# Light convolution and maxout MLP on one core: tokens loaded with their predecessors in one transfer, and a shorter weight split

## The chip, the cores and the metric

The kernel runs on one core of a Trainium2 chip. The metric is device time in microseconds (us) of one execution; the median of three runs of the kernel before is 1700.21 us (1697.39 to 1700.39). Engines are called as in the profile: PE (TensorE matmul) and PEld (its weight loads), DVE (VectorE), ACT (ScalarE), POOL (GpSimd), SP (SyncE, which here issues transfers and passes on waits).

## The reference

Inputs are `x` (8 x 4160 x 192) and `weight_gen` (8 x 4160 x 8 heads x 7 taps), 32-bit floats, and the weights `w1`, `w2`, `w3` (192 x 768) and `w_out` (768 x 192), which arrive as 64-bit floats.

```python
w = exp(weight_gen - max(weight_gen)); w = w / (sum(w) + 1e-9)       # over the 7 taps
out[b, s, h*24+g] = sum_k w[b, s, h, k] * x_pad[b, s + k, h*24+g]     # x_pad: 6 zero rows ahead of each batch
h = maximum(maximum(out @ w1, out @ w2), out @ w3)                    # 33280 tokens
result = h @ w_out
```

Each token is a weighted sum of itself and the six tokens before it in its batch, then a two-layer net with the maximum of three products as its nonlinearity.

## The kernel before, in words

**Tiling.** The 33280 tokens are laid on 128 partitions, 260 consecutive tokens on each, so that 16 partitions hold one batch. The work goes through 65 chunks of 4 tokens a partition (512 tokens). Loads and softmax are done by *super chunks*: super 0 is chunk 0 alone, each later one has three chunks. `load_super` (L183) brings a super's `weight_gen` rows and its tokens with the 6 preceding ones. For all supers but the first two the preceding tokens are on the same partition and one transfer of 128 rows brings everything (L191). In super 0 (and for two of the six in super 1) they are the last tokens of the partition before: a transfer of the super's own tokens (L197), 8 transfers of 15 partitions each for the rows ahead (L202), and a memset to zero (L196) for the partitions with which a batch begins.

**Stages of a chunk.** `softmax` (L210): maximum and sum on DVE, subtraction and multiplication on POOL, Exp on ACT. `product` (named x*c*.*t*, L246): on POOL, tap weights times tokens of token column *t*. `total` (+*c*.*t*, L261): sum over the taps on DVE. `transpose` (t*c*): channels onto partitions, by PE for chunks 0 to 2 (L276, L277), by DVE and ACT later. `parts` (p*c*, L300 to L309): the transposed values are split in a high and a low part in the reduced format that PE multiplies in. `up` (L343): for each of 9 steps (3 pairs of column blocks times 3 matrices) two accumulators of 9 products for each half of the 128 rows of PE; the three matrices' results are combined by a copy (ACT, L376) and two maxima (DVE, L378), then split in `h_hi` (ACT, L381) and `h_lo` (POOL, L385). `down` (L389): the second layer, 4 column blocks, for the chunk before.

**Splitting the weights.** The 64-bit weights are taken as pairs of 32-bit words. `split` (L453) makes from one unit of them a high and a low 32-bit float: |high word| on ACT (L470), a copy of the middle half words (L476), then DVE clamps (L481), shifts and masks (L483), puts the sign in (L488); ACT rounds to the high part (L493); DVE masks out the low mantissa (L494) and the exponent (L495), ACT scales the low part (L497) and POOL multiplies (L498). Units: a0 to a8 (256 elements; pair *jp* and matrix *i*), b0 to b2 (384 elements; the last 64 of the 192 input rows, whose high part ACT copies to both halves of `wb_hi`, L553, four copies a unit), d0 to d5 (192 elements, `w_out`). All of it happens while chunks 0 and 1 already run.

**Order.** The program is written out tick by tick: 22 ticks a chunk, 18 with half a step of `up` each and 4 (ticks 12 to 15) with `down` products. From chunk 5 on a table gives the tick of each stage. Before that, the list `OPENING` (L27) says at which tick which stage is issued, from -1 (before the first product); `stage` (L581) issues the next piece of it and, before that, whatever it depends on; `finish` issues the rest of a stage when it is due: p*c*, a*k* and b*k* at their step, all d at tick 34. Each engine works through its instructions in the order in which they are issued, so one that waits holds up all behind it on that engine. PE's accumulators, the transposed values and the split's work tiles share 8 PSUM banks (tag `ph`). A half of PE starts after a `nop` on SP has seen the other half's last product (L340), so SP's queue is on PE's way too. Loads go out on SP in program order (L558 to L566): s0 a0 b a1 s1 a2 d, the letters standing for a super, a pair's three matrices and the rest.

Of the kernel before, what the change touches and what calls it, by code (L numbers as in the profile page):

```python
# [13 lines left out]
F32 = mybir.dt.float32  # L14
F32R = mybir.dt.float32r
U32 = mybir.dt.uint32
U16 = mybir.dt.uint16
AF = mybir.ActivationFunctionType
ALU = mybir.AluOpType
# [4 lines left out]

OPENING = {  # L27
    -1: (
        "x0.0 x0.1 a0 a0 a1 a0 a1 x0.3 a2 a0 x0.2 a2 +0.0 a2 b0 b0 s1 +0.1 a1 a2 b0 +0.3 s1 "
        "a1 b0 s0 b1 +0.2 s1 a3 a3 a6"  # L30
    ),
    0: "a6 a3",
    1: "a6 b1 a5 t0 +1.0 a4 x1.2",
    2: "s0",
    3: "a3 x1.0 b1 a6 b2 a5",
    4: "a4 a5 t0",
    5: "a4 x1.1",
    6: "t0",
    7: "s0",
# [69 lines left out]
):  # L109

# [18 lines left out]


    assert NT % TC == 0
    chunks = [(t, TC) for t in range(0, NT, TC)]
    supers = [[0]]
    for c in range(1, len(chunks)):
        if len(supers) == 1 or len(supers[-1]) == SC:
            supers.append([])  # L150
        supers[-1].append(c)
# [18 lines left out]


    F_MAX = float(np.array(0x47EFFFFF, np.uint32).view(np.float32))
    F_MIN = float(np.array(0x38000000, np.uint32).view(np.float32))
    NU = 3 * P
    halves = (slice(0, DB), slice(DB, P))
    state = {}

    def pin(ins):

        tc.keep_in_program_order(ins)  # L180
        return ins

    def load_super(s):  # L183
        cs = supers[s]
        a = chunks[cs[0]][0]
        n = sum(chunks[c][1] for c in cs)
        xt = sup.tile([P, TS + PAD, D], F32, name="xt")
        wt = sup.tile([P, TS, H * K], F32, name="wt")
        pin(nc.sync.dma_start(out=wt[:, :n], in_=wf[:, a : a + n]))
        if a >= PAD:  # L190
            pin(nc.sync.dma_start(out=xt[:, : n + PAD], in_=xf[:, a - PAD : a + n]))  # L191
        else:


            z = PAD - a
            pin(nc.vector.memset(xt[:, :z], 0.0))  # L196
            pin(nc.sync.dma_start(out=xt[:, z : n + PAD], in_=xf[:, : a + n]))  # L197
# [8 lines left out]
        state["x", s], state["w", s], state["n", s] = xt, wt, n  # L206

    def softmax(s):  # L210
# [12 lines left out]
        yield  # L223
        pin(nc.vector.tensor_reduce(den, w3v, axis=AX.X, op=ALU.add))
        pin(nc.vector.tensor_scalar_add(den, den, 1e-9))
        pin(nc.vector.reciprocal(den, den))
        yield
# [6 lines left out]
    def product(c, t):  # L234
# [22 lines left out]
    def total(c, t):  # L257

        r = state.pop(("r", c, t))
        pin(  # L260
            nc.vector.tensor_reduce(  # L261
                state["acc", c][:, t], r, axis=AX.X, op=ALU.add
            )
        )

    def transpose(c):


# [42 lines left out]

    def after(ins, other):
# [26 lines left out]
    def up(step, half):  # L343
# [3 lines left out]
        for odd in range(2):  # L347
            j = 2 * jp + odd
            terms = [(wa_hi[:, j, i], xa_hi), (wa_hi[:, j, i], xa_lo), (wb_hi[:, j, i], xb)]
            if half == odd:  # L350
# [69 lines left out]

    clock = [0.0, 0.0]
# [25 lines left out]


    words = [w.bitcast(U32) for w in (w1, w2, w3, w_out)]

    def split(raw, hi, lo):  # L453

        high = raw[..., 1]


        n = int(np.prod(raw.shape[1:-1]))
        if 2 * n <= CH:
            both = ps.tile([P, CH], F32, name="ph")  # L460
            u, l = both[:, :n], both[:, n : 2 * n]
        else:
            u, l = (ps.tile([P, CH], F32, name="ph")[:, :n] for _ in range(2))
        e, f = (prep.tile([P, NU], F32, name=name, bufs=3)[:, :n] for name in ("e", "f"))
        f_words = f
        if len(raw.shape) == 4:
            u, l, e, f = (v.rearrange("p (i n) -> p i n", n=P) for v in (u, l, e, f))
        ui, li, ei = (v.bitcast(U32) for v in (u, l, e))

        pin(nc.scalar.activation(u, high.bitcast(F32), AF.Abs))  # L470
        yield


        flat = raw.rearrange("p i n w -> p (i n) w") if len(raw.shape) == 4 else raw
        pin(
            nc.scalar.copy(  # L476
                f_words.bitcast(U16).rearrange("p (n h) -> p n h", h=2),
                flat.bitcast(U16)[..., 1:3],
            )
        )  # L480
        pin(nc.vector.tensor_scalar(u, u, F_MAX, F_MIN, op0=ALU.min, op1=ALU.max))  # L481
        pin(
            nc.vector.tensor_scalar(  # L483
                ui, ui, 3, 0x3FFFF000, op0=ALU.logical_shift_left, op1=ALU.bitwise_and
            )
        )
        pin(
            nc.vector.scalar_tensor_tensor(  # L488
                ui, high, 0xC0000000, ui, op0=ALU.bitwise_and, op1=ALU.bitwise_or
            )  # L490
        )
        yield
        pin(nc.scalar.copy(hi, u))  # L493
        pin(nc.vector.tensor_scalar(li, f.bitcast(U32), 0x01FFFFFE, None, op0=ALU.bitwise_and))  # L494
        pin(nc.vector.tensor_scalar(ei, ui, 0xFF800000, None, op0=ALU.bitwise_and))  # L495
        yield
        pin(nc.scalar.activation(f, li, AF.Copy, scale=2.0**-36))  # L497
        pin(nc.gpsimd.tensor_tensor(lo, f, e, op=ALU.mult))  # L498


# [39 lines left out]
    def prepare_a(u):  # L540

        jp, i = divmod(u, 3)
        raw = raws_a[jp][:, i].rearrange("p (j n) w -> p j n w", j=2)
        pair = slice(2 * jp, 2 * jp + 2)
        yield from split(raw, wa_hi[:, pair, i], wa_lo[:, pair, i])

    def prepare_b(jp):
        raw = raw_b[:, jp]
        hi = prep.tile([P, 3, P], F32R, name="hi", bufs=1)
        yield from split(raw, hi, wb_lo[:, jp])  # L550
        for odd, h in enumerate(halves):
            for to in halves:
                pin(nc.scalar.copy(wb_hi[to, 2 * jp + odd], hi[h].bitcast(F32)))  # L553

    def prepare_down(j):
        yield from split(raw_down[:, j], wo[:, j, :D], wo[:, j, D:])

    state["now"] = -1  # L558
    load_super(0)
    load_up(0)  # L560
    load_rest()
    load_up(1)
    load_super(1)
    load_up(2)
    load_down()
    make_identity(nc, ident)  # L566


# [56 lines left out]
    for s, cs in enumerate(supers):  # L625
        ticks(cs[0], f"s{s}", SOFTMAX)
        if s > 1:
            at(max(TICKS * (cs[0] - LOAD[0]) + LOAD[1], 0), lambda s=s: load_super(s))
# [7 lines left out]
    for c in range(NC + 1):  # L636
        for tick in range(TICKS):
# [3 lines left out]
            if 2 * DOWN_AT <= tick < 2 * DOWN_AT + TC:  # L641
                if c == 1:
                    for j in range(NJ):
                        finish(f"d{j}")
                if 0 < c < NC:
# [5 lines left out]
            if odd == 0 and c == 0:  # L651
                finish(f"a{k}")
                finish(f"b{k // 3}")
            if c == NC:


# [48 lines left out]
```

## Time and profile before

| | before |
|---|---|
| runs, median (range) | 1700.21 us (1697.39 to 1700.39) |
| profiled execution, its own time | 1699.39 us |
| its span | 1697.6 us |
| PE, PEld busy | 1657.2, 1466.1 us |
| DVE, ACT, POOL busy | 1124.6, 1145.8, 1426.2 us |
| bytes moved | 79.51 MB, 47 GB/s on average |

The span runs from the first to the last event of the core; the profiled execution's own time has 1.8 us more around it. Rows of the views are read so: in a timeline, start and duration in us, engine, line, operation, what it writes and reads, and in brackets how long the engine was idle before it and what it waited for; in a grouping, count, busy us and mean ns of one, then idle time before them; in a list of transfers, issuing queue, count, KB each and the median us from issue to landing.

### The profile page before, as it was taken

What the parts mean: (1) busy time and instruction counts of PE and PEld (TensorE: products, weight loads), DVE (VectorE), ACT (ScalarE), POOL (GpSimd) and SP (SyncE); (2) the same over time, 40 slices, a digit from 0 to 9 for tenths busy, and PEclk for the clock granted to TensorE, in tenths of its full rate; (3) what the DMA queues carried; (4) which work ended last, traced back from release to release, by engine and by line L of the source; (5) the groups of instructions that cost most, each with busy time, mean ns of one, the idle gap of its engine ahead of it and who ended that gap; (6) DMA issues with size and microseconds to landing.
All of it is one profiled execution on the core that took longest, in us unless ns stands there. A gap on an engine that the chain in (4) does not pass through costs nothing.

```text
span 1697.6 us, 42191 instructions
## 1 busy us (share of the span) xinstructions
PE 1657.2 (98%) x16794; PEld 1466.1 (86%) x16794; DVE 1124.6 (66%) x1552; ACT 1145.8 (67%) x2896; POOL 1426.2 (84%) x844
## 2 busy tenths in 40 slices
PE   3899999999999999999999999999999999999999
PEld 2598889889889889889988988988988988988998
DVE  7966766666666666666666666666666666666653
ACT  5657667667666766766766766766776776676672
POOL 6888888989888888888888888988888888888872
PEclk9999999999999999999999999999999999999999
DMA  7010101101010110101010110101011010101000
GB/s 236 1 70 10 70 29 52 70 20 60 20 70 15 66 70 21 60 21 70 11 70 21 60 70 20 61 20 70 11 70 61 27 63 20 70 11 46 20 11 29
DMA packets 20422, 79.51 MB, mean 47 GB/s; under 512 B 2320, under 2 KB 5128, under 8 KB 17536
## 3 DMA queue, kind: packets, MB, share of 16 engines
q1 hardware_dynamic: 20104, 76.54, 11.9%
q8 instruction: 131, 2.15, 0.5%
q14 instruction: 67, 0.55, 0.1%
q10 hardware_dynamic: 120, 0.28, 0.0%
HBM read 51.25 MB, written 25.56 MB: 45 GB/s over the span
## 4 chain that ended last, share of the span: by engine, by line
PE 94%; DVE 3%; ACT 1%; DMA 1%; POOL 1%; SPq 0%; issue 0%; DVEq 0%
PE ph L329 94%; DVE acc L261 1%; DVE m L378 0%; DMA wt<-in_weight_gen_dram 0%; DVE ph L483 0%; POOL r L246 0%; DVE ph L488 0%; DVE e L495 0%; DVE ph L481 0%; DVE ph L494 0%; DMA xt<-in_x_dram 0%; SPq L529 0%; ACT room L290 0%; SPq L521 0%; POOL h_lo L385 0%
## 5 line engine op out<-in xcount | busy, mean ns | idle before, releaser
L246 POOL TENSOR_TENSOR r<-xt,wt 128x1344 f32<-128x1344 f32 x260 | 721.4, 2814 | 0.6 <-DMA xt<-in_x_dram 0.4
L378 DVE TENSOR_TENSOR m<-ph,m 128x512 f32<-128x512 f32 x780 | 520.6, 685 | 197.4 <-PE ph L329 113.7
L329 PE MATMUL ph<-xa_hi,wa_hi 64*128 64x512 f32 x2340 | 630.8, 391 | 9.4 <-DVE m L378 3.1
L385 POOL TENSOR_TENSOR h_lo<-m,h_hi 128x512 fp32r<-128x512 f32 x390 | 503.3, 1301 | 161.7 <-ACT h_hi L381 157.0
L329 PE MATMUL ph<-xa_lo,wa_hi 64*128 64x512 f32 x2340 | 626.9, 388 | 1.0 <-DVE xa_lo L304 1.0
L329 PE MATMUL ph<-xa_hi,wa_lo 64*128 64x512 f32 x2340 | 626.1, 387 | 1.1 <-POOL wa_lo L498 1.1
L329 PE MATMUL ph<-xb,wb_hi 64*128 64x512 f32 x2340 | 626.0, 387 | 0.0
L329 PE MATMUL ph<-wo,h_hi 64*128 64x384 f32 x3120 | 595.5, 355 | 0.0
L329 PE MATMUL ph<-wo,h_lo 64*128 64x192 f32 x3120 | 522.3, 247 | 0.0
L381 ACT CAST h_hi<-m 128x512 fp32r<-128x512 f32 x390 | 241.8, 621 | 409.7 <-DVE m L378 406.6
L261 DVE TENSOR_REDUCE acc<-r 128x192 f32<-128x1344 f32 x260 | 401.8, 1547 | 125.5 <-POOL r L246 125.5
L290 ACT COPY room<-room 32x128 f32<-32x128 f32 x1488 | 440.8, 296 | 25.7 <-DVE room L284 7.5
L329 PE MATMUL ph<-xc,wb_lo 64*128 64x512 f32 x1170 | 453.1, 387 | 0.1
L329 PEld LDWEIGHTS ph<-wo,h_lo 64*128 64x128 f32 x3120 | 398.8, 188 | 2.5
L329 PEld LDWEIGHTS ph<-wo,h_hi 64*128 64x128 f32 x3120 | 398.4, 184 | 2.9 <-issue 0.4
L329 PEld LDWEIGHTS ph<-xa_hi,wa_hi 64*128 64x128 f32 x2340 | 338.7, 185 | 53.9 <-DVE m L378 3.9
L329 PEld LDWEIGHTS ph<-xa_hi,wa_lo 64*128 64x128 f32 x2340 | 338.4, 185 | 42.0 <-POOL wa_lo L498 1.5
L329 PEld LDWEIGHTS ph<-xa_lo,wa_hi 64*128 64x128 f32 x2340 | 338.7, 185 | 38.7 <-DVE xa_lo L304 1.5
L329 PEld LDWEIGHTS ph<-xb,wb_hi 64*128 64x128 f32 x2340 | 338.7, 185 | 38.4 <-ACT xb L308 0.3
L376 ACT COPY m<-ph 128x512 f32<-128x512 f32 x390 | 221.8, 586 | 38.5 <-PE ph L329 35.3
L411 DVE TENSOR_TENSOR o<-ph,ob 128x192 f32<-128x192 f32 x260 | 86.7, 353 | 234.5 <-ACT ob L410 234.5
L329 PEld LDWEIGHTS ph<-xc,wb_lo 64*128 64x128 f32 x1170 | 216.3, 185 | 20.9 <-POOL wb_lo L498 0.5
(54 smaller groups left out, 702.6 us busy)
## 6 DMA issues: line engine op xcount, KB each, us to landing
xt<-in_x_dram SPq DMA_DIRECT2D x20, 1728.0 KB, 7.1
out_dram<-o SPq DMA_DIRECT2D x64, 384.0 KB, 2.3
wt<-in_weight_gen_dram SPq DMA_DIRECT2D x21, 336.0 KB, 3.0
h_hi<-in_moe_w_dram SPq DMA_DIRECT2D x6, 256.0 KB, 4.8
xt<-in_x_dram SPq DMA_DIRECT2D x1, 1536.0 KB, 9.3
h_lo<-in_moe_w_dram SPq DMA_DIRECT2D x6, 192.0 KB, 4.8
room<-in_moe_w_out_dram SPq DMA_DIRECT2D x1, 1152.0 KB, 8.1
xt<-in_x_dram SPq DMA_DIRECT2D x1, 960.0 KB, 5.2
```

The lines of the kernel that those rows point to most:

```text
L246: nc.gpsimd.tensor_tensor(r.rearrange("p (h g) k -> p k h g", g=G), xt[:, la + t : la + t + K].rearrange("p k (h g) -> p k h g", g=G), wt[ ...
L261: nc.vector.tensor_reduce(state["acc", c][:, t], r, axis=AX.X, op=ALU.add)
L290: pin(nc.scalar.copy(to[:, :, p : p + 32], blocks[p : p + 32, :, f : f + 32]))
L329: ins = nc.tensor.matmul(ph[:, :n], w[h], v[h], start=begins and half == 0 and q == 0, stop=ends and half == 1 and q == len(terms) - 1,)
L376: pin(nc.scalar.copy(m[:, :N], ph[:, :N]))
L378: pin(nc.vector.tensor_tensor(m[:, :N], ph[:, :N], m[:, :N], op=ALU.max))
L381: later(1, lambda: pin(nc.scalar.copy(hi, m[:, :N])))
L385: nc.gpsimd.tensor_tensor(lo, m[:, :N], hi.bitcast(F32), op=ALU.subtract)
L411: pin(nc.vector.tensor_tensor(o[:, t], po[:, :D], ob, op=ALU.add))
```

## The change

- **Tokens of supers 0 and 1.** One transfer brings partitions 1 to 127 with all their rows, the preceding ones included, which in memory lie just ahead; a second one brings partition 0. Partitions with which a batch begins get a batch's last tokens that way; these are set to zero afterwards, in super 0 by two DVE instructions that mask with `inside` (`clear`, 3 rows each), in super 1 by a transfer of zeros (`clear_by_dma`). Only partition 0's memset stays. All transfers of the opening go out on SP.
- **Super chunks.** Super 1 is chunk 1 alone (`FIRST = 2`); super 2 is loaded at tick 0.
- **Order of loads.** s0 a0 b s1 a1 a2 d (`LOADS`).
- **Split.** 12 units in place of 18: a0 to a5 of 256 or 512 elements, b0 to b2 of 384, d0 to d2 of 384. Six units (`WHOLE`) take |high word| times 2^-112 on ACT, the scaled low half word on ACT, a minimum on DVE, then two DVE instructions that shift and combine; the other six clamp with two Relu on ACT and have the two DVE instructions. The high part is rounded by ACT (d2: DVE), the low part is one subtraction, on POOL for a4, b0, b2, d0, otherwise on DVE. Each work tile keeps one PSUM bank.
- **b units.** The high part is written straight into one block of `wb_hi`, and its halves are swapped into the next block by two copies (b0, b1: by two transfers on SP); the second half of PE reads the block `j ^ 1`.
- **Softmax.** A dummy Exp on ACT at the start; the sums of supers 0 to 2 go to PSUM.
- **A new list** `OPENING`.

```diff
+        "x0.3 a0 x0.0 a0 a1 a0 a0 a0 b2 a1 +0.3 a1 a0 a1 x0.2 t0 s1 b2 x0.1 a1 a1 b2 b1 b1 "
+        "x1.2 b0 b0 b0 b2 b1 b0 s1 t0 t0 b2 b1 s0 a3 a2 a4 a5 a2 a3"
     ),
+    0: "b0 x1.1 p0 a3 a2 a3 s0 b2",
+    1: "a3 p0 a4 b1 a5 a5 a4 s2 b1 +1.1 a5 d0 d0 a1 b1 d0",
+    2: "s2 s1 d0 a4 s0 b1 a3 d2 a3 a5 a2 a5 d1 d0 a5 a4 s2 +1.0 x1.3 d1 d0 b2 +1.2",
+    8: "+1.3 d2 d1",
+    9: "d2 p1 t1 d1 a4 x2.2 p1 +0.2 t1 d0 d1 p0 p1 c0 +2.1 x2.3",
+    11: "b0",
+    19: "x2.0 +2.2",
+    20: "+2.3 d1",
+    22: "a2",
+    23: "d1",
+    27: "t2 s0 p2 s0 d2 d2 d2 d2 +0.1 b0 p2 t1 p2",
+    29: "+3.3",
+    31: "t3",
...
+LO_ON_POOL = ("a4", "b0", "b2", "d0")
+BY_DMA = ("b0", "b1")
+HI_ON_VECTOR = ("d2",)
+WHOLE = ("a0", "a1", "a2", "a4", "b1", "b2")
+FIRST = 2
+LOADS = "s0 a0 b s1 a1 a2 d"
+UNITS_A = ((0, 0, 1), (0, 1, 3), (1, 0, 2), (1, 2, 3), (2, 0, 2), (2, 2, 3))
+UNITS_D = ((0, 2), (2, 4), (4, 6))
...
             z = PAD - a
-            pin(nc.vector.memset(xt[:, :z], 0.0))
-            pin(nc.sync.dma_start(out=xt[:, z : n + PAD], in_=xf[:, : a + n]))
-            for b in range(B):
-                queue = nc.scalar if s == 0 and b % 2 else nc.sync
-                to = slice(b * PB + 1, (b + 1) * PB)
-                pin(
-                    queue.dma_start(
-                        out=xt[to, :z], in_=xf[to.start - 1 : to.stop - 1, NT - z :]
-                    )
-                )
+            rows = x.rearrange("b s d -> (b s) d")[NT - z : P * NT - z]
+            rows = rows.rearrange("(p t) d -> p t d", t=NT)[:, : n + PAD]
+            pin(nc.sync.dma_start(out=xt[1:, : n + PAD], in_=rows))
+            pin(nc.sync.dma_start(out=xt[:1, z : n + PAD], in_=xf[:1, : a + n]))
+            if s == 0:
+                pin(nc.vector.memset(xt[:1, :z], 0.0))
...
+    def clear(s):
+        n = PAD // 2
+        for t in (n, 0):
+            xs = state["x", s][:, t : t + n].rearrange("p t d -> p (t d)").bitcast(I32)
+            pin(
+                nc.vector.tensor_tensor(
+                    xs, xs, inside.broadcast_to([P, n * D]), op=ALU.bitwise_and
                 )
+            )
+            yield
...
+        if whole:
+            pin(nc.scalar.activation(low, halfwords[..., 1], AF.Copy, scale=7.49 / 65536))
...
+        if whole:
+            pin(eng.tensor_scalar(u, u, W_MAX, None, op0=ALU.min))
+            parts = (u.bitcast(U32), 3, low, ALU.logical_shift_left)
...
+                pin(nc.scalar.activation(u, upper, AF.Relu, bias=over, scale=-1.0))
+                yield
+                upper, bias, scale = u, span, -float(1 << 19)
+            pin(nc.scalar.activation(v.bitcast(U32), upper, AF.Relu, bias=bias, scale=scale))
+            parts = (low, 13, v.bitcast(U32), ALU.logical_shift_right)
...
+        eng = nc.gpsimd if name in LO_ON_POOL else nc.vector
+        pin(eng.tensor_tensor(lo, w, hi.bitcast(F32), op=ALU.subtract))
...
+        for h, to in zip(halves, reversed(halves)):
+            if f"b{jp}" in BY_DMA:
+                pin(nc.sync.dma_start(out=other[to].bitcast(F32), in_=hi[h].bitcast(F32)))
+            else:
+                pin(nc.scalar.copy(other[to], hi[h].bitcast(F32)))
...
+    for name in LOADS.split():
...
+    clear_by_dma(1, PAD - TC)
...
         if name[0] == "x":
             finish(f"s{super_of[c]}")
+            if c == 0 and t[0] == PAD // 2:
+                if "c0" not in running:
+                    stage("c0")
+            elif c == 0:
+                finish("c0")
```

More of the change, by code (lines that the diff above doesn't have):

```diff
@@ L17 @@
 U16 = mybir.dt.uint16
+I32 = mybir.dt.int32
 AF = mybir.ActivationFunctionType
@@ L169, in lightconv_maxout_kernel @@
     wo = const.tile([P, NJ, 2 * D], F32R, name="wo")
-    F_MAX = float(np.array(0x47EFFFFF, np.uint32).view(np.float32))
-    F_MIN = float(np.array(0x38000000, np.uint32).view(np.float32))
-    NU = 3 * P
+    E_MIN = (1023 - 127) << 4
+    E_MAX = (255 << 4) - 1
+    NU = 4 * P
+    edges = const.tile([P, P], F32, name="edges")
+    over, span, below, warm = (edges[:, k : k + 1] for k in range(4))
+    inside = edges[:, 4:5].bitcast(I32)
+    F_MAX = float(np.array((E_MIN + E_MAX) << 16 | 0xFFFF, np.uint32).view(np.float32))
+    W_MAX = float(np.array(255 << 20, np.uint32).view(np.float32) * (1 - 2.0**-24))
     halves = (slice(0, DB), slice(DB, P))
@@ L259, in total @@
         r = state.pop(("r", c, t))
+        if ("acc", c) not in state:
+            state["acc", c] = att.tile([P, TC, D], F32, name="acc")
         pin(
@@ L348, in up @@
             j = 2 * jp + odd
-            terms = [(wa_hi[:, j, i], xa_hi), (wa_hi[:, j, i], xa_lo), (wb_hi[:, j, i], xb)]
+            terms = [(wa_hi[:, j, i], xa_hi), (wa_hi[:, j, i], xa_lo)]
+            terms.append((wb_hi[:, j if half == 0 else j ^ 1, i], xb))
             if half == odd:
@@ L540, in prepare_a @@
     def prepare_a(u):
[L542 to L545, printed above, removed]
-    def prepare_b(jp):
[L548 to L553, printed above, removed]
@@ L555, in prepare_down @@
-    def prepare_down(j):
-        yield from split(raw_down[:, j], wo[:, j, :D], wo[:, j, D:])
-    state["now"] = -1
[L559 to L565, printed above, removed]
+        jp, a, b = UNITS_A[u]
+        flat = raws_a[jp][:, a:b].rearrange("p i n w -> p (i n) w")
+        to = (slice(None), slice(2 * jp, 2 * jp + 2), slice(a, b))
+        hi, lo = (w[to].rearrange("p j i n -> p i j n") for w in (wa_hi, wa_lo))
+        yield from split(flat, hi, lo, f"a{u}", "p (i j n) -> p i j n", j=2, n=P)
@@ new lines, in prepare_b @@
+    def prepare_b(jp):
+        flat = raw_b[:, jp].rearrange("p i n w -> p (i n) w")
+        hi, other = (wb_hi[:, 2 * jp + odd] for odd in range(2))
+        yield from split(flat, hi, wb_lo[:, jp], f"b{jp}", "p (i n) -> p i n", n=P)
+        yield
+        for h, to in zip(halves, reversed(halves)):
+            if f"b{jp}" in BY_DMA:
+                pin(nc.sync.dma_start(out=other[to].bitcast(F32), in_=hi[h].bitcast(F32)))
+            else:
+                pin(nc.scalar.copy(other[to], hi[h].bitcast(F32)))
@@ new lines, in prepare_down @@
+    def prepare_down(u):
+        js = slice(*UNITS_D[u])
+        flat = raw_down[:, js].rearrange("p j n w -> p (j n) w")
+        yield from split(flat, wo[:, js, :D], wo[:, js, D:], f"d{u}", "p (j n) -> p j n", n=D)
+    nc.gpsimd.iota(inside, pattern=[[0, 1]], base=0, channel_multiplier=1)
+    nc.vector.tensor_scalar(inside, inside, PB - 1, None, op0=ALU.bitwise_and)
+    nc.vector.tensor_scalar(inside, inside, 0, -1, op0=ALU.is_gt, op1=ALU.mult)
+    nc.gpsimd.memset(over, float(E_MIN + E_MAX))
@@ L566, in lightconv_maxout_kernel @@
+    nc.gpsimd.memset(span, float(E_MAX << 19))
+    nc.gpsimd.memset(below, float(-(E_MIN << 19)))
+    pin(nc.scalar.activation(warm, below, AF.Exp))
+    state["now"] = -1
+    for name in LOADS.split():
+        if name[0] == "s":
+            load_super(int(name[1:]))
+        elif name[0] == "a":
+            load_up(int(name[1:]))
+        else:
+            {"b": load_rest, "d": load_down}[name]()
     make_identity(nc, ident)
+    clear_by_dma(1, PAD - TC)
     NC = len(chunks)
@@ L626, in lightconv_maxout_kernel @@
         ticks(cs[0], f"s{s}", SOFTMAX)
-        if s > 1:
+        if f"s{s}" not in LOADS.split():
             at(max(TICKS * (cs[0] - LOAD[0]) + LOAD[1], 0), lambda s=s: load_super(s))
@@ L642, in lightconv_maxout_kernel @@
                 if c == 1:
-                    for j in range(NJ):
-                        finish(f"d{j}")
+                    for u in range(len(UNITS_D)):
+                        finish(f"d{u}")
                 if 0 < c < NC:
@@ L651, in lightconv_maxout_kernel @@
             if odd == 0 and c == 0:
-                finish(f"a{k}")
+                finish(f"a{[(k // 3, k % 3) in [(jp, i) for i in range(a, b)] for jp, a, b in UNITS_A].index(True)}")
                 finish(f"b{k // 3}")
```

157 lines of the change are left out of this document (66 added, 91 removed), and 10 rows, old and new, of the table OPENING.

## The prediction

> **What bounds the kernel now.** I read the page first: its span and the chain that ended last.
>
> ```profile
> span 1697.6 us, 42191 instructions
> PE 94%; DVE 3%; ACT 1%; DMA 1%; POOL 1%; SPq 0%; issue 0%; DVEq 0%
> ```
>
> The profiled execution took 1699.39 us, 1.8 us more than its span and 0.8 us under the 1700.21 us median of the three timed runs. TensorE carries 94% of the chain, so I asked for busy time by stage, to see where it does not.
>
> ```profile
> core 0: us, PE busy (x) PEld busy (x) DVE busy (x) ACT busy (x) POOL busy (x), PEclk, DMA share, GB/s
> 0.00:30.00 30.00, 2.71 (x9) 1.21 (x9) 21.89 (x40) 14.56 (x31) 18.51 (x19) 1.00 0.81 253
> 30.00:82.00 52.00, 42.57 (x277) 28.35 (x279) 49.81 (x96) 35.48 (x83) 42.45 (x32) 0.97 0.12 47
> 90.00:170.00 80.00, 79.97 (x811) 71.35 (x808) 54.34 (x71) 53.04 (x134) 67.14 (x39) 1.00 0.11 43
> 170.00:1694.00 1524.00, 1523.82 (x15604) 1357.69 (x15604) 993.97 (x1340) 1038.43 (x2640) 1291.83 (x754) 1.00 0.11 43
> ```
>
> Read the last two rows first: from 90 us on PE is never without work, at 811/80 = 10.1 and 15604/1524 = 10.2 matmuls a us. None of that work changes in amount. In the row 30:82 PE makes 277/52 = 5.3 a us while VectorE (DVE) is busy 49.81 of 52 us: there DVE sets the pace. Before 30 us PE has next to nothing. So the change can act only on when PE starts and on how fast DVE gets through its list; what arrives later at the end of this opening, ends later by as much. Two rows of the timeline mark its ends: the first product of chunk 0, and the first down product (tick 34), from about which PE no longer waits.
>
> ```profile
> 29.96 0.79 PE L329 MATMUL ph<-xa_hi,wa_hi 64*128 64x512 f32 x1 [2.82 <-ACT xa_hi L300]
> 81.86 0.44 PE L329 MATMUL ph<-wo,h_hi 64*128 64x384 f32 x1
> ```
>
> **The token load in one piece.** This is the part that decides. Before, super chunk 0's tokens come as 128 rows of 4 tokens (L197) and 8 transfers of 15 rows (L202). Afterwards one transfer brings 127 rows of 10 tokens, 127 x 7,680 B = 952.5 KB (KB of 1024 B); super chunk 1 gets another of the same size. What does it cost? The nearest rows are the 128-row loads of the list of DMA issues, and the queue that carried only four of the 15-row ones.
>
> ```profile
> q10 hardware_dynamic: 120, 0.28, 0.0%
> xt<-in_x_dram SPq DMA_DIRECT2D x20, 1728.0 KB, 7.1
> xt<-in_x_dram SPq DMA_DIRECT2D x1, 960.0 KB, 5.2
> xt<-in_x_dram ACTq DMA_DIRECT2D x4, 67.5 KB, 3.9
> 1.18 0.42 SPq L197 DMA_DIRECT2D xt<-in_x_dram  x1
> 7.84 7.65 POOL L246 TENSOR_TENSOR r<-xt,wt 128x1344 f32<-128x1344 f32 x3 [0.40 <-DMA xt<-in_x_dram]
> ```
>
> The 960 KB row is the same load with one row more: 5.2 us if the 127 rows spread over the 16 DMA engines as 128 do. That is the lower bound. For the upper one, take the difference of the two big loads: 768 KB more took 1.9 us more, so each of 16 engines moved 48 KB in 1.9 us, 25.3 KB/us. One engine alone would need 952.5/25.3 = 37.7 us, and 5.2 - 60/25.3 = 2.8 us lie around any load: 40.5 us. Which end? The ACT queue's row counts 120 packets for 4 transfers, 30 each: 15 rows, and 15 more that I read as one completion per engine. A 15-row transfer so ran on 15 engines, one row each; 128 rows make 8 for each of 16. Every transfer here is an even deal of rows. 127 is prime: no count from 2 to 16 deals it evenly. An uneven deal (8 rows on fifteen engines, 7 on one) occurs nowhere here and is not excluded either. I take the even deal, one engine, and keep the other end as the first rival.
>
> The Trainium skill, page "DMA: Bandwidth & Descriptors", section "Why a DMA increments its semaphore by 16 and not by 1", says that the hardware takes the largest number of engines up to 16 that divides the row counts of both sides, and names 127 rows as a case of one engine. The 15-row transfers agree with it; no run shown here has 127 rows. By that rule the sum is the 1753 us below, without it 1687 us.
>
> Now the order of the loads counts. I take it that an engine serves its shares in the order of issue; an ordinary load is then complete only when the busy engine's sixteenth of it is through, too.
>
> ```profile
> h_hi<-in_moe_w_dram SPq DMA_DIRECT2D x6, 256.0 KB, 4.8
> h_lo<-in_moe_w_dram SPq DMA_DIRECT2D x6, 192.0 KB, 4.8
> raw_a<-in_moe_w_dram SPq DMA_DIRECT2D x3, 256.0 KB, 3.0
> wt<-in_weight_gen_dram SPq DMA_DIRECT2D x2, 112.0 KB, 2.7
> ```
>
> New order: s0 a0 b s1 a1 a2 d. Tokens of s0: 1.2 + 40.5 = 41.7 us; the first product (POOL, 7.84 us before) and all that follows wait for it, and DVE too, whose clearing of the first rows stands ahead of every split. Shares of a0 (3 x 256 KB), b (6 x 192) and s1's weights (112): (768 + 1152 + 112)/16 = 127 KB, 5.0 us: 46.7. Tokens of s1: 37.7 more: 84.4. Shares of a1 and a2, 48 KB or 1.9 us each: 86.3 and 88.2.
>
> Who waits for a1 and a2? The list puts the first stages of units a3, a2, a4 and a5 ahead of p0, so they stand on ScalarE's (ACT) queue ahead of xa_hi, which releases the first matmul.
>
> ```profile
> L470 ACT ACTIVATE ph<-raw_a 128x256 f32<-128x256 f32 x3 | 1.2, 399 | 0.0
> L476 ACT COPY f<-raw_a 128x512 uint16<-128x512 uint16 x3 | 1.8, 614 | 0.0
> L376 ACT COPY m<-ph 128x512 f32<-128x512 f32 x10 | 5.7, 585 | 0.2 <-PE ph L329 0.2
> L300 ACT CAST xa_hi<-ph 128x512 fp32r<-128x512 f32 x2 | 1.2, 590 | 0.4 <-PE ph L276 0.4
> L246 POOL TENSOR_TENSOR r<-xt,wt 128x1344 f32<-128x1344 f32 x13 | 34.9, 2722 | 0.5 <-DMA xt<-in_x_dram 0.4
> L498 POOL TENSOR_TENSOR wb_lo<-f,e 128x384 fp32r<-128x384 f32 x3 | 3.0, 1009 | 1.4 <-DVE e L495 1.4
> ```
>
> From 86.3: a3 and a5 (256 wide) 0.40 + 0.61 each, a2 and a4 (512 wide) 2 x 0.585 each, one Relu taken as 0.40: 4.8 us, then xa_hi 0.59: first matmul at 91.7 instead of 29.96, **+61.7 us**. There is a second hold at the same place. POOL's queue has x1.2, x1.1, b2's and b0's low parts in this order; x1.2 needs s1's tokens: 84.4 + 2 x 2.72 + 2 x 1.01 = 91.9 for b0's low part, the fourth term of the very first product. If the weights came early, this would remain.
>
> **The split and the rest of the list.** From the first matmul to the first down product took 81.86 - 29.96 = 51.9 us, paced by DVE. I count DVE's list for that stretch in both orders (before up to the second maximum of chunk 1's fifth step, where the 52 us end; afterwards up to tick 30, whose maxima free the banks that the down products take).
>
> ```profile
> L261 DVE TENSOR_REDUCE acc<-r 128x192 f32<-128x1344 f32 x12 | 18.3, 1543 | 0.0
> L378 DVE TENSOR_TENSOR m<-ph,m 128x512 f32<-128x512 f32 x18 | 11.9, 682 | 0.1
> L481 DVE TENSOR_SCALAR ph<-ph 128x256 f32<-128x256 f32 x9 | 3.8, 424 | 2.4 <-ACT ph L470 2.4
> L481 DVE TENSOR_SCALAR ph<-ph 128x192 f32<-128x192 f32 x6 | 2.1, 355 | 0.0
> L481 DVE TENSOR_SCALAR ph<-ph 128x384 f32<-128x384 f32 x3 | 1.7, 559 | 0.5 <-ACT ph L470 0.5
> L224 DVE TENSOR_REDUCE den<-wt 128x96 f32<-128x672 f32 x1 | 0.8, 843 | 0.0
> L226 DVE RECIPROCAL den<-den 128x96 f32<-128x96 f32 x1 | 0.8, 752 | 0.0
> ```
>
> Each old split is five DVE instructions. Left after 29.96 us: 25 of 256, 10 of 384, 30 of 192 elements: 25 x 0.424 + 10 x 0.559 + 30 x 0.355 = 26.9 us. The new split has 2 to 4, since the clamp is one minimum or two Relu on ACT, the exponent word is gone, and the low part is one subtraction, on POOL for four units. Left in the stretch: 7 of 512 (priced as L378), 6 of 256, 11 of 384: 7 x 0.682 + 6 x 0.424 + 11 x 0.559 = 13.5 us. That is -13.4. Against it: one sum more (+1.5), two parts of chunk 2 (+1.4, as L378), the second half of super 2's softmax (+1.6); two maxima fewer (-1.4). Net -10.3. I take **-9 us**, leaving 1.3 us for new short waits: half of wb_hi for b0 and b1 now comes by a DMA behind SP's other issues, and two units hold a PSUM bank from tick 2 to ticks 23 and 27. Bounds: 0 and -14.
>
> Edits at nothing: clearing two blocks of 576 elements instead of the two memsets, about 1 us of DVE hidden in the wait for the tokens; the early Exp table load, hidden there too; ACT's twelve Relu, less the copies dropped, beside 35.48 busy of 52 us (if ACT had no room, 12 x 0.40 = 4.8 us); super 1 of one chunk and super 2 loaded at tick 0: from 90 us on PE covers it, and DVE, busy 54.34 of 80 us, has room.
>
> Sum: 61.7 - 9 = +52.7: 1699.39 + 52.7 = 1752.1 on the profile's scale, **1753 us** on the median's.
>
> **The rivals.** *The 127 rows spread over all engines* (chance 0.16): the tokens land at 1.2 + 5.2 = 6.4 us, products start near 7.8 as before, a1 and a2 are long there. Then the DVE relief is the whole story: -9 in the stretch, and a first matmul earlier by about 4 us, since it no longer stands behind a stage of a split:
>
> ```profile
> 29.05 0.37 ACT L493 CAST wa_hi<-ph 128x256 fp32r<-128x256 f32 x1 [1.59 <-DVE ph L488]
> 4.02 1.28 ACT L222 ACT_TABLE_LOAD   x1 [4.02 <-DVE red L215]
> ```
>
> (1.6 us of that wait and the 1.3 us table load leave the path, and the splits ahead of the start are shorter by 1 to 2 us). 1700.2 - 13 = 1687 us, own range 1682 to 1696. It decides if the tokens land before some 20 us: each us of landing beyond 7 takes one of the 13. For it: nothing here forbids an uneven deal. Against it: none is seen.
>
> *Spread, but the relief is eaten* (0.03): ACT takes over from DVE as the bound of 30:82 with its 4.8 us, and the banks held through tick 27 cost PE the rest: 1697 to 1703 us. For it: ACT already has 35.48 of 52 us there; against it, 16.5 us free.
>
> *One engine* (0.81) is the forecast. Its own bounds: an engine alone may be up to 40% faster than one beside fifteen others, which takes 11 us from each of the two token loads: 1731; at the 0 bound of the relief (+9), with SP's issues held up by the slow load for some us twice and a lower rate (388 GB/s were the most that a 2 us window showed, row below, 23.7 KB/us an engine, +2.5 us twice): 1775.
>
> ```profile
> 30.00:32.00 2.00, 0.96 (x2) 0.45 (x3) 1.86 (x5) 1.95 (x5) 2.00 (x2) 1.00 1.11 388
> ```
>
> **How the numbers follow.** About 0.2% (3.4 us) is what a measurement of this kernel can tell from no change. Slower: 0.81 and a share of the third case, 0.82. Same 0.02, faster 0.16. The range has to hold 8 in 10, and the one-engine case alone has 0.81: so I give it nearly whole, its bounds widened by 5 us at each end, 1726 to 1780.
>
> **What would show it.** Right: in the list of DMA issues the 952.5 KB tokens land some 40 us after issue, the first product starts near 42 us, the second load lands near 84, the first L329 matmul near 92 after a wait of ACT for raw weights; PE has next to no work in the first two of 40 slices; the stretch to the first down product is 42 to 45 us, with DVE still above 90% in it. Wrong: a landing of 5 to 9 us (first rival); a second load that lands early; a stretch near 52 us (the split is then not the relief); a DVE that waits for ACT's Relu in it (third case).

## The result and the profile after

| | before | after |
|---|---|---|
| median of the runs made together | 1699.38 us (1697.39 to 1700.39) | 1753.78 us (1753.11 to 1754.24) |
| profiled execution, its own time | 1699.39 us | 1753.34 us |
| its span | 1697.6 us | 1751.5 us |

The ratio is 1.0321, with a 95% interval of 1.0303 to 1.0339: the changed kernel is 54.4 us slower, and 1753 us was foreseen. The page of the kernel after, its span, two of the slices and its chain:

```profile
span 1751.5 us, 42087 instructions
...
PE   0079999999999999999999999999999999999999
...
PE 94%; DMA 3%; SPq 2%; DVE 0%; ACT 0%; issue 0%
```

A slice is 44 us. In the first two PE does next to nothing, and the chain has 2% in SP's queue and 3% in transfers, where before it had DVE, ACT and POOL. The same kernel's busy time in stretches that are cut at its own marks (start, length, then busy us and instructions of each engine, the clock, the DMA share, GB/s):

```profile
0.00:42.00 42.00, 0.00 (x0) 0.00 (x0) 2.66 (x7) 1.88 (x3) 2.01 (x12) 1.00 0.18 57
60.00:90.00 30.00, 0.00 (x0) 0.00 (x0) 0.00 (x0) 0.18 (x1) 1.98 (x1) 1.00 0.26 80
94.69:137.84 43.15, 38.60 (x277) 29.99 (x279) 41.06 (x57) 28.09 (x54) 40.90 (x23) 1.00 0.23 87
```

Twice, for 42 and for 30 us, the engines do next to nothing and the core moves 57 and 80 GB/s, where before's first 30 us had 253. SP's own queue in the same kernel shows a hold that the prediction had only among its bounds:

```profile
1.18 0.32 SPq L169 DMA_DIRECT2D xt<-in_x_dram  x1
1.55 16.76 SPq L170 DMA_DIRECT2D xt<-in_x_dram  x1
18.35 5.18 SPq L531 DMA_DIRECT2D h_hi<-in_moe_w_dram  x3
23.57 20.28 SPq L539 DMA_DIRECT2D h_lo<-in_moe_w_dram  x6
44.53 0.29 SPq L169 DMA_DIRECT2D xt<-in_x_dram  x1
44.99 17.16 SPq L170 DMA_DIRECT2D xt<-in_x_dram  x1
```

L169 is the transfer of 127 rows; it is issued in 0.3 us. Issuing the one-row transfer behind it takes 16.76 us, the six loads of b 20.28 us, so that the second load of 127 rows goes out at 44.53 us, after the first has landed. (The raw weights lie in tiles of other names: a0 and a1 land in `h_hi`, b in `h_lo`, a2 in `raw_a`, d in `room`; `xt<-ident` is `clear_by_dma`.) Three timelines of the kernel after, put in order: DVE's clearing and POOL, then ACT and PE at the start of the matmuls.

```profile
42.03 1.43 DVE L181 TENSOR_TENSOR xt<-xt,edges 128x576 int32<-128x576 int32 x2 [36.67 <-DMA xt<-in_x_dram]
```

```profile
42.92 8.10 POOL L228 TENSOR_TENSOR r<-xt,wt 128x1344 f32<-128x1344 f32 x3 [36.84 <-DVE xt L181]
...
88.02 2.60 POOL L228 TENSOR_TENSOR r<-xt,wt 128x1344 f32<-128x1344 f32 x1 [33.50 <-DMA xt<-in_x_dram]
95.24 2.65 POOL L228 TENSOR_TENSOR r<-xt,wt 128x1344 f32<-128x1344 f32 x1 [4.63 <-DMA xt<-ident]
```

```profile
89.82 0.40 ACT L456 ACTIVATE ph<-h_hi 128x256 f32<-128x256 f32 x1 [35.09 <-DMA h_hi<-in_moe_w_dram]
...
94.05 0.58 ACT L283 CAST xa_hi<-ph 128x512 fp32r<-128x512 f32 x1
```

```profile
94.69 0.79 PE L308 MATMUL ph<-xa_hi,wa_hi 64*128 64x512 f32 x1 [35.48 <-ACT xa_hi L283]
...
99.77 0.79 PE L308 MATMUL ph<-xc,wb_lo 64*128 64x512 f32 x1 [1.79 <-POOL wb_lo L507]
...
137.84 0.33 PE L308 MATMUL ph<-wo,h_hi 64*128 64x384 f32 x1
```

Read in order of time: super 0's tokens hold DVE and POOL up to 42 us, super 1's tokens hold POOL up to 88 us, the weights a1 behind them hold ACT up to 89.8 us, and xa_hi, behind nine ACT instructions on the same queue, lets PE begin at 94.69 us instead of 29.96. The first down product comes at 137.84 us instead of 81.86.

The difference of the spans, 1751.5 - 1697.6 = 53.9 us, so has three parts: +64.7 us to the first matmul (94.69 - 29.96), -8.8 us from there to the first down product (43.15 against 51.90), and -2.0 us after it, the rest. In the last, the steady state, both kernels issue their output transfers in the same period of 75.56 us for three chunks (rows of both below, with the experiments).

### The profile page after: what moved, and what is told of

Read it like the earlier page. It is cut to its first block, busy times and chain, and to the rows that moved or that the text cites. A ratio compares the mean times of both kernels' runs of the same rounds, so it can differ in the third digit from the quotient of the medians.

```text
span 1751.5 us, 42087 instructions
## 1 busy us (share of the span) xinstructions
PE 1651.3 (94%) x16794; PEld 1641.1 (94%) x16794; DVE 1110.3 (63%) x1504; ACT 1136.7 (65%) x2862; POOL 1418.2 (81%) x834
## 4 chain that ended last, share of the span: by engine, by line
PE 94%; DMA 3%; SPq 2%; DVE 0%; ACT 0%; issue 0%
PE ph L308 94%; SPq L170 2%; DMA h_hi<-in_moe_w_dram 1%; DMA h_lo<-in_moe_w_dram 1%; SPq L531 0%; DVE ph L483 0%; DVE ph L490 0%; ACT low L458 0%; ACT ph L456 0%; PE ph L259 0%; ACT low L462 0%; ACT xc L289 0%; PE ph L260 0%; DVE red L199 0%; DVE acc L245 0%
## 5 line engine op out<-in xcount | busy, mean ns | idle before, releaser
L308 PE MATMUL ph<-xa_hi,wa_hi 64*128 64x512 f32 x2340 | 623.2, 389 | 37.3 <-ACT xa_hi L283 35.5
L308 PE MATMUL ph<-wo,h_lo 64*128 64x192 f32 x3120 | 551.8, 247 | 0.0
L308 PEld LDWEIGHTS ph<-wo,h_lo 64*128 64x128 f32 x3120 | 458.6, 188 | 0.0
L308 PEld LDWEIGHTS ph<-wo,h_hi 64*128 64x128 f32 x3120 | 453.7, 184 | 0.0
L308 PEld LDWEIGHTS ph<-xa_hi,wa_hi 64*128 64x128 f32 x2340 | 358.2, 184 | 40.0 <-ACT xa_hi L283 35.9
L308 PEld LDWEIGHTS ph<-xa_lo,wa_hi 64*128 64x128 f32 x2340 | 357.4, 185 | 2.1 <-DVE xa_lo L287 1.1
L308 PEld LDWEIGHTS ph<-xb,wb_hi 64*128 64x128 f32 x2340 | 357.3, 184 | 2.0 <-ACT wb_hi L504 0.8
L308 PEld LDWEIGHTS ph<-xa_hi,wa_lo 64*128 64x128 f32 x2340 | 357.3, 184 | 1.5 <-issue 0.4
## 6 DMA issues: line engine op xcount, KB each, us to landing
xt<-in_x_dram SPq DMA_DIRECT2D x2, 952.5 KB
```

Of the source, the lines that this page charges most:

```text
L308: ins = nc.tensor.matmul(ph[:, :n], w[h], v[h], start=begins and half == 0 and q == 0, stop=ends and half == 1 and q == len(terms) - 1,)
```

## The experiments

The theory is that a transfer of 127 rows runs on one DMA engine, and that this happens twice, each time holding all that is behind it. The rivals are that the source pattern, the order of loads, the clearing, the list or the split is the cause, or that only one of the two loads counts. Times of the kernel before, run together with each group, were 1697.86 to 1698.72 us.

**112 + 15 rows.** Both numbers can be dealt evenly, to 16 and to 15 engines; all else is the kernel after.

```diff
-            pin(nc.sync.dma_start(out=xt[1:, : n + PAD], in_=rows))
+            for b, e in PIECES[s]:                      # PIECES = (((1, 113), (113, 128)),) * 2
+                pin(nc.sync.dma_start(out=xt[b:e, : n + PAD], in_=rows[b - 1 : e - 1]))
```

> The kernel after, with the tokens of supers 0 and 1 brought in two transfers each, 112 rows and 15 rows, in place of one of 127. Theory (a row count that no number from 2 to 16 divides goes to one DMA engine, and this is the whole loss): the tokens land within 7 us of their issue, SP's issues are no longer spread out, the first matmul comes near 26 us, the first down product some 43 us later, and the time is about 1687 us (1682 to 1696). Rival (what costs the time is the new source pattern, the new order of loads, the clearing or the new split): the time stays above 1730 us.

1686.25 us (1685.10 to 1687.17), 0.9928 of before (0.9914 to 0.9943). Its PE timeline and its own stretch from first matmul to first down product:

```profile
27.16 0.79 PE L310 MATMUL ph<-xa_hi,wa_hi 64*128 64x512 f32 x1 [1.66 <-ACT xa_hi L285]
...
71.07 0.33 PE L310 MATMUL ph<-wo,h_hi 64*128 64x384 f32 x1
```

```profile
27.16:71.07 43.91, 39.72 (x277) 30.15 (x279) 41.06 (x57) 28.09 (x54) 40.76 (x23) 1.00 0.26 95
```

One number in one line, 127, cost 67.5 us; all the rest of the change together gains 12 us. The rival falls. The tokens took a little longer than the 7 us expected: 7.5 us (median) for 112 rows, 7.8 for 15. DVE's 57 instructions and 41.06 us in the stretch are those of the kernel after to the digit.

**Only super 0 dealt evenly.** Super 1's tokens stay one transfer of 127 rows.

```diff
+PIECES = (((1, 113), (113, 128)), ((1, 128),))
```

> Only super 0's tokens come as 112 + 15 rows; super 1's stay one transfer of 127 rows, in its place ahead of a1 and a2. Theory (each of the two slow loads costs by itself, the second by holding the weights a1 and a2 that are queued behind it and chunk 1's products): super 1's tokens are issued near 13 us and land near 51, a1 and a2 some 3 us later, the first matmul comes near 60 us, and the time is about 1718 us (1710 to 1726). Rival (only the load from which all products start counts, the second is hidden as chunk 1 is needed late): about 1688 us.

1719.92 us (1718.91 to 1720.26), ratio 1.0126 (1.0111 to 1.0141). POOL and PE of this kernel:

```profile
53.73 2.60 POOL L230 TENSOR_TENSOR r<-xt,wt 128x1344 f32<-128x1344 f32 x1 [32.95 <-DMA xt<-in_x_dram]
```

```profile
60.42 0.79 PE L310 MATMUL ph<-xa_hi,wa_hi 64*128 64x512 f32 x1 [34.95 <-ACT xa_hi L285]
```

Super 1's load went out at 10.72 us (13 expected) and its tokens were in use at 53.73 (51). Each load costs by itself: 33.7 us the second (1719.92 - 1686.25), 33.9 us more the first (1753.78 - 1719.92).

**The slow load last.** As before it, with super 1's 127 rows issued behind a1, a2 and d.

```diff
-LOADS = "s0 a0 b s1 a1 a2 d"
+LOADS = "s0 a0 b a1 a2 d s1"
```

> As the run with only super 0 dealt evenly, and super 1's 127 rows are moved to the end of the loads, behind a1, a2 and d. Theory (there is a second hold: POOL has x1.2 and x1.1 queued ahead of the low parts of b2 and b0, and the very first product needs b0's): super 1's tokens land near 56 us, b0's low part comes near 64, and though a1 and a2 land before 20 us the time stays near 1718 us (1710 to 1728). Rival (the weights' lateness is the only hold): 1690 us or below 1695.

1719.37 us (1719.20 to 1720.08), ratio 1.0123 (1.0106 to 1.0140): the same time, by another way. PE and POOL of this kernel:

```profile
31.66 0.76 PE L310 MATMUL ph<-xa_hi,wa_hi 64*128 64x512 f32 x1 [0.50 <-ACT xa_hi L285]
...
66.00 0.79 PE L310 MATMUL ph<-xc,wb_lo 64*128 64x512 f32 x1 [31.09 <-POOL wb_lo L509]
```

```profile
58.95 5.12 POOL L230 TENSOR_TENSOR r<-xt,wt 128x1344 f32<-128x1344 f32 x2 [32.43 <-DMA xt<-in_x_dram]
64.00 1.95 POOL L509 TENSOR_TENSOR wb_lo<-w,wb_hi 128x384 fp32r<-128x384 f32 x2
```

The weights are early and the first matmul comes at 31.66 us, 29 us earlier than in the run before this one. It gains nothing, since the fourth term needs wb_lo, which POOL makes behind two products of super 1's tokens: PE waits 31.09 us for it, until 66.00. That is the second hold of the prediction, shown alone: the order of loads cannot cure it.

**Even and uneven deals.** Super 0 in 125 + 2 rows, super 1 in 126 + 1.

```diff
+PIECES = (((1, 126), (126, 128)), ((1, 127), (127, 128)))
```

> The kernel after, with super 0's tokens in transfers of 125 and 2 rows, super 1's in transfers of 126 and 1. Theory (an even deal: the largest number of engines up to 16 that divides the rows): 125 rows go to 5 engines and land 10 us after issue, 126 go to 14 and land some 6 us after issue; the time is 1689 to 1694 us. First rival (rows that are no multiple of 16 and over 16 go to one engine): both take about 40 us, the time is near 1753 us. Second rival (an uneven deal is allowed and 127 is a case by itself): both land within 7 us, 1686 us.

One run, 1692.39 us. The issues on SP, and who waited for them:

```profile
1.19 0.66 SPq L171 DMA_DIRECT2D xt<-in_x_dram  x2
...
16.91 0.72 SPq L171 DMA_DIRECT2D xt<-in_x_dram  x2
```

```profile
14.09 1.43 DVE L183 TENSOR_TENSOR xt<-xt,edges 128x576 int32<-128x576 int32 x2 [8.77 <-DMA xt<-in_x_dram]
```

```profile
27.05 2.63 POOL L230 TENSOR_TENSOR r<-xt,wt 128x1344 f32<-128x1344 f32 x1 [0.25 <-DMA xt<-in_x_dram]
```

The 125 rows, with the 2 and the 1 beside them, had landed 12.9 us after issue (10 were expected), the 126 after at most 10.1 us, with other loads beside them (6 were expected); neither took 40. So it is not that any number but a multiple of 16 goes to one engine. Between the other two theories the time decides less well: 12.9 us are nearer the 10 of five engines than the 5 of sixteen, and 1692.39 us lies in the theory's range (1689 to 1694); the packet counts below settle it. The Trainium skill, page "DMA: Bandwidth & Descriptors", section "Why a DMA increments its semaphore by 16 and not by 1", has the rule of the largest divisor; the order 127, 125, 126 of these landings agrees with it.

**Another queue: ACT.** The two transfers of 127 rows are issued by ACT.

```diff
-            pin(nc.sync.dma_start(out=xt[1:, : n + PAD], in_=rows))
+            pin(nc.scalar.dma_start(out=xt[1:, : n + PAD], in_=rows))
```

> The kernel after, with the two transfers of 127 rows issued by ACT in place of SP. Theory A (the one DMA engine is the hold: it serves the shares of all queues in the order of their issue): a0 and b still land near 42 us and the time is 1745 to 1757 us. Theory B (the queue is the hold: behind another queue's slow transfer nothing waits): SP's issues follow each other at about 0.5 us, a0 and b land within 10 us of issue and a1 and a2 before 30; super 0's tokens still land near 42 and super 1's near 80, so that b0's low part comes near 88 and the time is about 1743 us (1735 to 1750).

One run, 1754.26 us, which is A's time, but neither theory holds as it was put. SP's queue, ACT with its own queue, and POOL:

```profile
22.77 27.91 SPq L531 DMA_DIRECT2D h_hi<-in_moe_w_dram  x3
50.73 1.38 SPq L531 DMA_DIRECT2D raw_a<-in_moe_w_dram  x3
90.93 0.38 SPq L545 DMA_DIRECT2D room<-in_moe_w_out_dram  x1
```

```profile
14.20 0.22 ACTq L169 DMA_DIRECT2D xt<-in_x_dram  x1
...
68.39 0.40 ACT L456 ACTIVATE ph<-raw_a 128x256 f32<-128x256 f32 x1 [1.99 <-DMA raw_a<-in_moe_w_dram]
```

```profile
51.26 8.08 POOL L228 TENSOR_TENSOR r<-xt,wt 128x1344 f32<-128x1344 f32 x3 [34.58 <-DVE xt L181]
...
91.03 2.59 POOL L228 TENSOR_TENSOR r<-xt,wt 128x1344 f32<-128x1344 f32 x1 [28.19 <-issue]
```

SP's issues are held for 27.91 us though no slow transfer is on its queue: against B, and the first product starts at 51.26 us, 8 us later than with SP. ACT read a2's last matrix at 68.39 us and POOL super 1's tokens only at 91.03, though they had been issued by 14.42 us (14.20 + 0.22) and a2 from 50.73 on: this speaks against a strict order of issue, hence against A. For POOL's last wait the profile names no releaser; that it was for these tokens is inferred from what the product reads. What exactly holds an issuing queue stays open.

**Another queue: POOL.** The same with `nc.gpsimd`.

> The kernel after, with the two transfers of 127 rows issued by POOL (GpSimd) in place of SP. The Trainium skill, page DMA: Bandwidth & Descriptors, section on why a DMA increments its semaphore by 16, names an exception for this queue: some direct copies of 127 rows are put on all 16 engines, 8 rows on most. Theory A (the rule is the queue's, and this one deals unevenly): the tokens land within 10 us of issue, SP's issues are not held, and the time is 1686 to 1695 us, the more the longer POOL needs to issue. Theory B (127 rows go to one engine on this queue too): about 1750 us (1742 to 1758).

1689.31 us (1688.86 to 1690.33), ratio 0.9948 (0.9932 to 0.9963). The transfer in this kernel's list, and its issue on POOL:

```profile
xt<-in_x_dram POOLq DMA_DIRECT2D x2, 952.5 KB, 10.5
```

```profile
1.47 1.23 POOL L169 DMA_DIRECT2D xt<-in_x_dram  x2 [0.40 <-issue]
```

The same 127 rows land in 10.5 us (median) where SP's took about 40, and POOL spends 1.23 us on issuing both. The exception that the Trainium skill names for this queue (page "DMA: Bandwidth & Descriptors", the section quoted above) agrees. It takes one word in the source to have most of what 112 + 15 rows give.

How the rows were dealt can be counted, by the reading that the prediction made of ACT's 15-row transfers: a packet for each row and one completion for each engine. The queues of these kernels (packets, MB, share of the time); q1 is SP's in the kernel after, with 112 + 15, with 125 + 2 and 126 + 1, and with the loads on ACT, then ACT's own and POOL's:

```profile
q1 hardware_dynamic: 20076, 77.27, 11.5%
q1 hardware_dynamic: 20136, 77.27, 12.3%
q1 hardware_dynamic: 20096, 77.27, 12.2%
q1 hardware_dynamic: 19820, 75.31, 11.4%
q10 hardware_dynamic: 256, 1.95, 0.3%
q0 software_dynamic: 288, 1.95, 0.5%
```

On ACT's queue the two loads make 256 packets, and SP's has 256 fewer: 127 rows and one completion each, so one engine. 112 + 15 rows, twice, make 60 packets more, 254 rows and 62 completions, as 2 x (16 + 15) engines give. 125 + 2 and 126 + 1 make 20 more, 22 completions, as 5 + 2 + 14 + 1 give: each the largest number up to 16 that divides the rows. POOL's 288 are 34 more than the rows, so not one engine a transfer.

**The load alone, in the kernel before.** Super 0's tokens come in 127 + 1 rows and are cleared with a mask; nothing else is changed. First the mask lay in a tile of 4 bytes a partition, then in one of 512.

```diff
+    inside = const.tile([P, 1], F32, name="inside")     # second run: [P, P], of which one column is used
...
+                pin(nc.sync.dma_start(out=xt[1:, : n + PAD], in_=rows))
```

> The kernel before, with one thing of the change: super 0's tokens and the rows ahead of them come as one transfer of 127 rows and one of 1 row, followed by the clearing with a mask; split, list, chunks and order of loads are those of before. Theory: the tokens land near 41 us after the start, the first product starts near 42 instead of 7.84, the first matmul comes about 34 us later than before's 29.96, and the time is about 1733 us (1725 to 1740). Rival (the transfer is hidden or spread, and the loss belongs to the new list or split): 1698 to 1703 us.

1773.58 us (1773.02 to 1774.08), 40 us more than expected. The first matmul comes at 66.17 us, 36.2 us later than before's (34 were foreseen). But the whole steady state is slower. SP's output transfers in before and in this run (start and length of groups of three):

```profile
273.43 50.70 SPq L419 DMA_DIRECT2D out_dram<-o  x3
348.99 50.71 SPq L419 DMA_DIRECT2D out_dram<-o  x3
```

```profile
314.07 51.88 SPq L434 DMA_DIRECT2D out_dram<-o  x3
391.39 51.88 SPq L434 DMA_DIRECT2D out_dram<-o  x3
```

348.99 - 273.43 = 75.56 us for three chunks before, 77.32 us here; the kernel after has 75.56 us, too:

```profile
352.60 50.71 SPq L399 DMA_DIRECT2D out_dram<-o  x3
428.16 50.71 SPq L399 DMA_DIRECT2D out_dram<-o  x3
```

> The kernel before with super 0's tokens in 127 + 1 rows, as in the run that came out at 1773.58 us, but the mask lies in a tile of 512 bytes a partition in place of one of 4 bytes. In that run the first matmul came 36.2 us later than before's, as foreseen, and yet every period of three chunks took 77.32 us in place of 75.56. Theory (the 4-byte tile moves all tiles behind it off their old addresses, and TensorE reads them more slowly): the period is 75.56 us again and the time about 1734 us (1728 to 1740). Rival (the late start itself leaves the steady state out of step): the period stays 77.3 us and the time near 1773 us.

1736.57 us (1734.55 to 1737.35), ratio 1.0223 (1.0207 to 1.0239); the period is 75.56 us, the first matmul comes at 66.05 us, 36.1 us later than before's, and the span of 1734.2 us is 36.6 us above before's. So the load alone, in the other kernel, costs the late start and nothing else, and the 37 us on top came from the tile of the mask.

> The kernel before with one thing added: a tile of 4 bytes a partition, set to zero by POOL at the start and read by nobody, in the place where the mask lay. Theory (the addresses of the tiles behind it are the cause of the slower period): the period of three chunks is 77.3 us in place of 75.56, the matmuls of 512 columns take 393 ns in place of 387, the start is unchanged, and the time is about 1737 us (1733 to 1741). Rival (it was something else in the kernel with the mask): 1697 to 1701 us.

The edit is one line ahead of `halves`, in the kernel before:

```diff
+    nc.gpsimd.memset(const.tile([P, 1], F32, name="pad"), 0.0)
```

1734.78 us (1734.12 to 1735.43), ratio 1.0215 (1.0201 to 1.0229), with a period of 77.32 us. The same group of matmuls, in before and here (count, busy us, mean ns, then the idle time before them):

```profile
L329 PE MATMUL ph<-xb,wb_hi 64*128 64x512 f32 x2340 | 626.0, 387 | 0.0
```

```profile
L330 PE MATMUL ph<-xb,wb_hi 64*128 64x512 f32 x2340 | 649.0, 392 | 0.0
```

PE waits for nothing here either; in the records each matmul takes longer. A tile that nobody reads costs 36 us.

> The kernel before with the same unused tile of POOL, but 64 bytes a partition in place of 4 (which take 32 in the built program). Theory (what counts is whether the tiles behind it begin at a multiple of 64 bytes, as before's do; 32 bytes move them half a step off): the period is 75.56 us and the time 1697 to 1701 us. Rival (any move of these tiles costs, and the 512 byte mask was a lucky one): the period stays near 77.3 us and the time near 1735 us.

1713.64 us (1713.30 to 1715.08), ratio 1.0090 (1.0073 to 1.0107), and a period of 76.30 us: neither what 64 bytes as the unit would give nor what any move would. So 32, 64 and 512 bytes more ahead of the tiles cost 1.76, 0.74 and 0 us in each period. The weights' tiles (`wa_hi` to `wo`) are made ahead of the added one and keep their places, so it is the tiles behind that moved. Which of these it is, why their place counts, and where between 64 and 512 bytes the loss ends, was not tried.

**Where the gain of the split lies.** The six units with two Relu get a minimum on DVE and one Relu on ACT instead, with 112 + 15 rows.

```diff
-CLAMP_ON_VECTOR = ()
+CLAMP_ON_VECTOR = ("a3", "a5", "b0", "d0", "d1", "d2")
```

> The kernel after with the tokens in 112 + 15 rows, and the clamp of the six units that use two Relu done by a minimum on DVE and one Relu on ACT. Theory (DVE sets the pace between the first matmul and the first down product, so that this is where the new split gains): six more DVE instructions, two of 256 and four of 384 elements, 2 x 0.42 + 4 x 0.56 = 3.1 us more on DVE, and the time goes from 1686.25 us to 1688 to 1690 us. Rival (ACT, with its Relu, has become the bound there): 1683 to 1686 us.

1686.91 us (1686.22 to 1688.32), ratio 0.9934 (0.9922 to 0.9947), which is between the two and not to be told from the 1686.25. Its stretch from first matmul to first down product:

```profile
26.41:71.40 44.99, 38.90 (x279) 29.86 (x281) 43.19 (x62) 25.87 (x50) 41.05 (x23) 1.00 0.25 93
```

DVE has 2.1 us more in it, but the stretch is only 1.1 us longer, so that DVE's work shows in its length in part. The first matmul comes 0.75 us earlier; a1's transfer was there earlier, too: ACT began its stage at 21.03 us, and at 22.25 with 112 + 15 rows alone, after a wait of 1.22 us for it. So the run does not decide between theory and rival, and the second Relu is worth nothing that can be measured.

**A version without POOL's wait for the zeros.** With 112 + 15 rows, x1.1 and x1.3 change places in the list, with their sums, so that no product ahead of b0's low part needs the cleared rows.

```diff
-    0: "b0 x1.1 p0 a3 a2 a3 s0 b2",
+    0: "b0 x1.3 p0 a3 a2 a3 s0 b2",
...
```

> The kernel after with the tokens in 112 + 15 rows, and x1.1 and x1.3 (with their sums) change places in the list, so that no product ahead of b0's low part waits for the clearing of super 1's first two tokens. Theory (POOL's 3.6 us wait for that clearing holds the fourth term, and PE with it, by about 1 us): b0's low part comes 3 to 4 us earlier and the time is 1 to 2 us below the 1686.25 of the 112 + 15 rows alone: 1684 to 1685.5 us. Rival (DVE sets the pace of this stretch and the wait is covered): 1686 to 1687 us.

1685.89 us (1685.49 to 1686.49), ratio 0.9926 (0.9914 to 0.9939). The first matmul comes at 26.06 us instead of 27.16, which the edit does not explain: ACT found a1's transfer landed at 21.11 us instead of 22.25. The fourth term comes at 29.63 instead of 31.66, the first down product at 69.9 instead of 71.07. So the stretch between is as long as before, 43.8 and 43.91 us, which is what the rival says; the gain in the time, 0.4 us, is within what two groups of runs differ by. This and the plain 112 + 15 rows are faster than both kernels.

## Why the prediction was right, step by step

**What bounds the kernel** held: what the opening lost, the end lost, and apart from the 2.0 us below nothing in 1600 us of saturated PE gave it back.

**One engine for 127 rows** held. Super 0's tokens were in use at 42.03 us (41.7 foreseen), 40.9 us after issue (40.5). That the two loads are the whole loss is shown by 112 + 15 rows; that it is one engine, and that the divisor is what counts, by the packet counts. No run shows the 40% by which the lower bound let an engine alone be faster: with the 2.8 us that were put around any load, 952.5 KB took 38 us, 25 KB/us, against 25.3 taken.

**The second load** was mis-sized by 3.6 us: 84.4 foreseen, 88.02 measured. The step that failed took the shares to run through without a gap. But SP itself was held, issued the load at 44.53 us, and from there it took 43.5 us more, 43.0 and 43.3 in the two runs where only this load had 127 rows. From it to a1 the 1.9 us foreseen were 1.8 (89.82).

**From a1 to the first matmul** 5.4 us were foreseen, 4.87 measured. So +64.7 us instead of +61.7.

**The second hold** was named and is shown by the run with the slow load last. Its size was off: b0's low part was foreseen at 91.9 us and done at 99.7. 3.6 us of that are the load; 4.63 us are a wait that the prediction missed: x1.1 reads the rows that `clear_by_dma` sets to zero, and that transfer stands on SP behind all loads. It cost PE 1.79 us, inside the stretch, where 1.3 us had been left for such waits.

**The split** was right: -8.75 us measured in the stretch (51.90 to 43.15), -9 foreseen. The same stretch of before reads

```profile
29.96:81.86 51.90, 42.47 (x275) 28.25 (x275) 49.72 (x96) 35.52 (x83) 42.35 (x32) 0.97 0.12 48
```

96 DVE instructions have become 57, and DVE's busy time 49.72 us has become 41.06, -8.66; its idle time, 2.18 and 2.09 us, stayed, so that it is 95% busy, as foreseen. The list in the prediction gave -10.3. The missing 1.6 us are not the waits it was cut for: the durations of neighbouring instructions overlap a little, so a sum over many short ones takes off too much. Added up one by one they are 55.1 us before and 44.7 after, -10.4, as in the list; the busy time, which counts an overlap once, fell by 8.66. That DVE set the pace rests on this stretch, where the length fell with DVE's busy time; the run with the clamp on DVE shows it only in part.

**After the first down product** nothing was foreseen, and 2.0 us were gained (1.6 with 112 + 15 rows). In the 100 us behind it the records have 1010 matmuls before and 1027 after: at that mark before's PE was not yet at its full pace. That the total came out within 1.2 us (1752.1 foreseen on the profile's scale, 1753.34 measured) so rests on luck, too: two misses of 2 to 3 us that cancel.

**The first rival**, 127 rows spread over all engines, gave 1687 us; with rows that do spread the time is 1686.25, of which -2.8 us at the first matmul (-4 foreseen), -8.0 in the stretch (-9) and -1.6 behind it. Of the second rival there is no sign: ACT has 28.09 busy of 43.91 us in that stretch.

## What to carry to other kernels

Before a load whose number of partitions is no multiple of 16 goes out on SP's or ACT's queue, look for the largest number up to 16 that divides it, and cut the load in two where that is small: 112 + 15 rows here saved 67.5 us against 127. A load on the critical path is judged with everything queued behind it, on its own queue and on the engines whose lists stand behind its first reader, since moving it last can leave the time as it was. When an edit shifts every tile behind it, compare the period of the steady state before blaming the edit itself.

## What the runs showed of the hardware that was not expected

Issues behind a slow transfer were held: the next, of one row, took 16.76 and 17.16 us to issue, and SP was held for 27.91 us even when the slow transfers were ACT's; by what is open. The same 127 rows that took about 40 us from SP's queue took 10.5 us from POOL's.

The place of the tiles in the on-chip memory changed TensorE's pace: 32 bytes more ahead of them made matmuls of 512 columns about 5 ns longer (392 instead of 387 in the rows above), the period 2.3% longer and the kernel 36 us slower, 64 bytes made it 15 us slower, and 512 bytes did nothing. The changed kernel's own new constant, `edges`, takes 512 bytes a partition and keeps the period of 75.56 us.
